# Step 0 of a convolution and MLP kernel: weight blocks rounded once and copied between partitions, their split moved behind the first product

## The chip, the core and the metric

The kernel runs on one core of one Trainium2 chip. The metric is the device time of one execution in microseconds. The core's engines have an instruction stream each: PE multiplies matrices (and loads weights, PEld), DVE does vector arithmetic, ACT activations, scaled copies and copies out of PE's accumulators, POOL further vector work, and it issues software DMA transfers; SP issues hardware DMA transfers. Instructions of one stream start in order, so one that waits holds up all behind it.

## The reference

Two layers: a causal convolution of 7 taps along the sequence, whose taps are a softmax over each head's weights, then an MLP of two products with a sigmoid-approximated GELU between them, all in float32.

```python
w = np.exp(weight - np.max(weight, axis=-1, keepdims=True))
w = w / (np.sum(w, axis=-1, keepdims=True) + 1e-09)          # (8 heads, 7 taps)
x = np.einsum('hk,bskhg->bshg', w, x_unf).reshape(B * S, D)  # B = 8, S = 4096, D = 192
h = x @ w_in                                                 # (32768, 192) @ (192, 2048)
g = h * (1.0 / (1.0 + np.exp(-1.702 * h)))
out = g @ w_out                                              # (32768, 2048) @ (2048, 192)
```

## The kernel before

**Steps.** The 32768 tokens go through in 32 steps of 1024 (`big` 0 to 31), each two sequences of 512 tokens, laid out in two halves of 256 (`o` = 0 and 1). The 192 channels are three chunks of 64 (`NC`, the index `k` or `c`); half 0 of the tokens has its channels on partitions 0 to 63, half 1 on 64 to 127 (`halves[o]`). So each weight that multiplies both halves must stand on both sets of partitions. The 2048 hidden columns are 16 blocks of 128 (`NF`, the index `r` or `i`), two neighbouring ones a pair (`N_W` = 8 pairs, index `j`).

**What a step does.** `transpose_x` (L143, DVE) brings x to channel-major, `conv` (L160 and L162, DVE) sums the taps into `own`. `hidden` runs 16 *units*, one for each block r: `unit` makes block r of the first product in a PE slot, `gelu` (L240, ACT) empties it into `g`; four slots are there. Then the second product turns `g` into the output, DVE transposes it (`turn`), SP stores it (L496).

**Steps 1 to 31.** A unit is three passes (`pass_of`, L209) of six matmuls on values split in parts: `xh` with `wh`, `xl` with `wl` (even r) or a ring slot (odd r), `xd` with a ring slot. `wh` and `wl` stay in SBUF; the other three of each pair are read back from `w_dram` into seven ring slots by SP (`load_ring`, L196) in every step. The second product of these steps (`second`) is a scheme with fewer products on sums of blocks (a hand-written list, `PLAN`); it needs sums and differences of blocks of w_out: the *forms*, 25 of them, 17 not being blocks themselves.

**Step 0** does plain float32 products and prepares all that. `split` (L387 to L391: two TENSOR_SCALAR of DVE, two activations of ACT) takes a loaded piece of a weight apart into words, `round_w_in` and `round_w_out` (L395, L398, L406, DVE) put it together rounded. A piece is 128 x 768 words: a pair of blocks of w_in, or four blocks of w_out. In the loop over `i` of `first_step`, after each `plain(slot, ...)` (L233, six matmuls), the next pair is rounded, then the last one split: `split_w_in` (L427 on ACT gives `wh`, L428 on POOL the rest), `split_rest` (L433 on DVE gives `wl` and a ring slot, L436 on POOL two more ring slots, L438 on SP writes the three slots to `w_dram`). As the ring is also where the parts are staged, a slot is free again only when its write has landed. `second_plain` (L499) is the second product of step 0, 48 rows of eight matmuls from `w_out_s`; behind each row it calls `at(row)`, into which the conv of step 1 (in `own`, which is free when the first product ends) and the forms are put. The forms: `add_forms` copies blocks on ACT (L296 and its neighbours) and lets POOL add others to them by accumulating DMAs (L298); `end_forms` turns four signs on ACT (L302). After `second_plain` come unit 0 of step 1, the output of step 0, and `hidden` of step 1. With the copies out of `second_plain`'s slots (L516, ACT) its slots come free.

**Order.** Nothing is scheduled: each engine runs its instructions in the order in which this code writes them, and a tile framework adds the waits that the data need. On SP stand, in order: x of step 0, sixteen loads of w_in (two for each pair: the same rows to both halves of the partitions), x of step 1 (eight transfers), pieces of w_out and the writes of L438, the first seven ring loads, x of step 2.

Raw words are loaded where there is room before the first step needs it: `raw` (in `g`, `osbs`, `room`), `raw_out` (`room`, `osbs`), and the words that are being rounded stand in four `sets` of the forms' tile.

Of the kernel before, what the change touches and what calls it, by code (L numbers as in the profile page):

```python
# [8 lines left out]
F32 = mybir.dt.float32  # L9
# [7 lines left out]
def kernel(  # L17
# [9 lines left out]
    nc = tc.nc  # L27
# [120 lines left out]
    def conv_src(c, k):  # L148
        return xt[:, c, :, Q - PAD + k : Q - PAD + k + T]
# [4 lines left out]
    def own_of(c):  # L154
        return own[:, 2 * c : 2 * c + 2, :]

    def conv(c, k, times=vec.tensor_scalar_mul):
        src, dst, tap = conv_src(c, k), own_of(c), tap_of(c, k)
        if k == 0:
            times(dst, src, tap)  # L160
        else:
            vec.scalar_tensor_tensor(  # L162
                out=dst, in0=src, scalar=tap, in1=dst, op0=ALU.mult, op1=ALU.add
            )

    def split_high(b0, b1):
        act.mul(xh[:, b0:b1, :], own[:, b0:b1, :], NEAR)

    def split_low(b0, b1):
        vec.scalar_tensor_tensor(  # L170
            out=xl[:, b0:b1, :], in0=own[:, b0:b1, :], scalar=UP, in1=wide(xh[:, b0:b1, :]),
            op0=ALU.mult, op1=ALU.subtract,
        )

    def split_both(b0, b1):
        vec.tensor_sub(xd[:, b0:b1, :], wide(xh[:, b0:b1, :]), own[:, b0:b1, :])
# [3 lines left out]
    wh = consts.tile([P, NF, NC, P], F32R)  # L180
# [5 lines left out]
    w_dram = dram.tile([STREAM, P, NC * P], F32)  # L186

# [18 lines left out]
    def pass_of(slot, w, t, first=False, last=False):  # L206
        for k in KS:
            for o in range(2):
                nc.tensor.matmul(  # L209
                    slot[o], w[halves[o], k, :], t[halves[o], 2 * k : 2 * k + 2, :],  # L210
                    start=first and k == KS[0], stop=last and k == KS[-1], skip_group_check=True,
                )

    def upper_high(slot, r):
        pass_of(slot, wh[:, r], xh, first=True)

    def upper_low(slot, r, big):
        if r % 2:
            q = STREAM * big + place("l", r)
            pass_of(slot, in_ring(q), xl)  # L220
            later(q)
        else:
            pass_of(slot, wl[:, r // 2], xl)

    def lower(slot, r, big):
        q = STREAM * big + place("d", r)
        pass_of(slot, in_ring(q), xd, last=True)
        later(q)

    def plain(slot, w):  # L230
        for k in KS:
            for o in range(2):
                nc.tensor.matmul(  # L233
                    slot[o], w[halves[o], k, :], own[halves[o], 2 * k : 2 * k + 2, :],
                    start=k == KS[0], stop=k == KS[-1], skip_group_check=True,
                )
# [29 lines left out]
    def form(i):  # L266
# [8 lines left out]
    COPY_O = [  # L275
        [(10, 2), (16, 1), (17, 0), (18, 0), (8, 7), (9, 5), (11, 3, -1), (12, 6, -1)],
        [(13, 3), (14, 3), (15, 0), (19, 4), (20, 4), (21, 5), (22, 7)],
        [],
        [(23, 1), (24, 1)],
        [(1, 14), (7, 0, -1)],  # L280
    ]
    SUMS_O = [
# [5 lines left out]
    ]  # L288
    TURN_O = (9, 17, 20, 21)

    def add_forms(stage):
        for dst, src, *sign in COPY_O[stage]:
            if sign:
                act.mul(form(dst), form(src), -1.0)
            else:
                act.copy(form(dst), form(src))  # L296
        for dst, src in SUMS_O[stage]:
            nc.gpsimd.dma_start(out=form(dst), in_=form(src), accum_op=ALU.add)  # L298

    def end_forms():  # L300
        for i in TURN_O:
            act.mul(form(i), form(i), -1.0)  # L302
# [7 lines left out]
    at_room, at_osbs = ([t[:, 2 * PART * i : 2 * PART * (i + 1)] for i in range(n)] for t, n in ((flat_room, 3), (osbs, 1)))  # L310
    raw = [flat_g(r)[:, 2 * PART * i : 2 * PART * (i + 1)] for r in range(3) for i in range(2)]
    raw += at_osbs + at_room[0:1]
    raw_out = at_room + at_osbs
    sets = [flat_form[:, 2 * PART * i : 2 * PART * (i + 1)] for i in range(4)]
    words_in, words_out = sets[0:3], (sets[3], sets[0])
    assert 8 * PART <= FORMS * NG * HD
    diag = flat_room[:, 2 * PIECE : 2 * PIECE + 2 * K * P].rearrange("p (c k q) -> p c k q", c=2, k=K)
# [19 lines left out]
    def load_w_in(j):  # L337
        for o in range(2):
            nc.sync.dma_start(
                out=raw[j][halves[o], :].bitcast(U32).rearrange("p (k f) -> p k f", k=NC), in_=w_in_v[j]  # L340
            )
# [7 lines left out]
    load_w_in(0)  # L349
    for j in range(1, N_W):  # L350
        load_w_in(j)
# [26 lines left out]
    def in_part(j):  # L378
        return raw[j], words_in[j % 3]

    def out_piece(i):
        return raw_out[i], words_out[(1, 0, 1, 0)[i]]
# [32 lines left out]
    def round_w_in(j):  # L415
        piece = in_part(j)
        join(piece)
        lo, hi, m, e = words(piece)
        rounded(piece, [(lambda a: a, m.bitcast(F32))])

    def w_of(j, what="w"):
        lo, hi, m, e = words(in_part(j))
        t = (m if what == "w" else e).bitcast(F32)
        return t.rearrange("p (k r f) -> p r k f", k=NC, r=2)

    def split_w_in(j):
        act.mul(wh[:, 2 * j : 2 * j + 2], w_of(j), DOWN)  # L427
        nc.gpsimd.tensor_sub(w_of(j, "rest"), w_of(j), wide(wh[:, 2 * j : 2 * j + 2]))  # L428

    def split_rest(j):  # L430
        lows = wl[:, j], in_ring(place("l", 2 * j + 1))
        for h in range(2):
            vec.tensor_scalar_mul(lows[h], w_of(j, "rest")[:, h], C)  # L433
        for h in range(2):
            r = 2 * j + h
            nc.gpsimd.tensor_sub(in_ring(place("d", r)), wide(lows[h]), wide(wh[:, r]))  # L436
        for q in range(3 * j, 3 * j + 3):
            nc.sync.dma_start(out=w_dram[q], in_=wide(in_ring(q)).rearrange("p k f -> p (k f)"))  # L438
# [134 lines left out]
    def second(big, bx, bs, by, more, next_first):  # L573
# [53 lines left out]
        def if_more(split):  # L627
            if more:
                split(0, 2 * NC)
# [18 lines left out]
    def first_step(tiles):  # L648
# [13 lines left out]
        act.copy(own_of(1), pairs[1][0].rearrange("p (n t) -> p n t", n=2))  # L662
        act.copy(own_of(2), pairs[1][1].rearrange("p (n t) -> p n t", n=2))
        load_x(1)
        for i in (1, 2):
            load_w_out(i)

        for i in range(NF):
            slot = tiles[i % 4]
            j = i // 2  # L670
            plain(slot, w_of(j)[:, i % 2])
            if i % 2 == 0:
                if j + 1 < N_W:
                    round_w_in(j + 1)
                split_w_in(j)
                if j + 2 < N_W:
                    split(in_part(j + 2))
                if i == 12:
                    load_w_out(3)
                if i == 14:  # L680
                    split(out_piece(1))
                    load_w_out(0)
            else:
                split_rest(j)
                if i == 15:
                    split(out_piece(2))
                if i in (7, 9, 11):
                    transpose_x(1, (i - 7) // 2)
            gelu(slot, i)

        pf, pa, pb, pc = tiles[3], tiles[1], tiles[0], tiles[2]

        for q in range(STREAM, STREAM + RING):
            load_ring(q)
        round_w_out(1)
        split(out_piece(3))
        round_w_out(2)
        split(out_piece(0))
        round_w_out(3)
        round_w_out(0)  # L700
        load_x(2)

        n_last = 3 * NG * NG - 1

        def at(i):
            if i == 0:
                for c in range(NC):
                    conv(c, 0, times=act.mul)
                for c in range(NC):
                    for k in range(1, K):  # L710
                        conv(c, k)
                split_high(0, 2 * NC)
                split_low(0, 2 * NC)
                split_both(0, 2 * NC)
                for c in range(NC):
                    transpose_x(2, c)
            if i == 2:
                add_forms(0)
            if i == 10:
                add_forms(1)  # L720
            if i == 20:
                add_forms(2)
                add_forms(3)
            if i == n_last:
                add_forms(4)
                end_forms()
# [62 lines left out]
```

## Time and profile before

| | |
|---|---|
| time, median of 3 runs | 2220.69 us (2220.56 to 2221.07) |
| the profiled execution | 2219.38 us, of which the profile's span 2217.7 us |
| mean granted PE clock | 0.991 |
| PE busy | 2181.6 us, 98% of the span |
| PEld | 1519.3 us, 69% |
| DVE | 1793.5 us, 81% |
| ACT | 1004.9 us, 45% |
| POOL | 376.6 us, 17% |
| software DMA queue / hardware DMA queue | 31.9% / 30.0% of 16 engines' span |
| chain that ended last | PE 93%, DMA 3%, DVE 1%, POOL 1% |

Busy shares are means over the whole span; of its 40 slices of 55.4 us the first has PE at 7 tenths, the next two at 8, all others at 9 or more. In rows of instructions, "L233" is line 233 of the kernel, `out<-in` the names of what is written and read, then sizes, then how many alike in a row; in brackets the idle time of the engine before them and what ended it. A row of a stretch gives, for each engine, busy time and number of instructions.

### The profile page before, as it was taken

How to read it: one execution, taken by the hardware profiler on the slowest of the kernel's cores; microseconds unless marked ns; L12 is line 12 of the kernel's file. 1: busy time of each engine (PE TensorE's matmuls, PEld its weight loads, DVE VectorE, ACT ScalarE, POOL GpSimd, SP SyncE). 2: the span in 40 equal slices, each digit the busy share in tenths (PEclk: the TensorE clock that was granted, in tenths of full speed). 3: DMA queues.
4: the chain of work that ended last, by engine and by line, in shares of the span. 5: the costliest groups of instructions: out<-in, count | busy, mean ns of one | idle time of the engine just before them, and what ended most of it. 6: DMA issues, size and time to landing. Idle time of an engine off the chain costs nothing.

```text
span 2217.7 us, 66206 instructions
## 1 busy us (share of the span) xinstructions
PE 2181.6 (98%) x28898; PEld 1519.3 (69%) x28898; DVE 1793.5 (81%) x2488; ACT 1004.9 (45%) x2133; POOL 376.6 (17%) x478
## 2 busy tenths in 40 slices
PE   7889999999999999999999999999999999999999
PEld 3457677766677766677766677766777766777766
DVE  7948888888888888888888888888888888888856
ACT  4444444444444444444444444444444444444443
POOL 3441111111111111011111011111011111011000
PEclk8899999999999999999999999999999999999999
DMA  9486575656575666575656575666575665675554
GB/s 226 134 167 154 126 183 150 163 144 145 137 184 147 164 146 149 135 180 148 166 145 144 143 178 147 165 148 142 144 175 147 166 146 139 152 174 147 137 120 98
DMA packets 269633, 338.41 MB, mean 153 GB/s; under 512 B 121504, under 2 KB 231520, under 8 KB 269344
## 3 DMA queue, kind: packets, MB, share of 16 engines
q0 software_dynamic: 44656, 144.19, 31.9%
q1 hardware_dynamic: 223040, 189.61, 30.0%
q8 instruction: 226, 3.70, 0.7%
q10 hardware_dynamic: 1648, 0.39, 0.1%
q14 instruction: 63, 0.52, 0.1%
HBM read 202.57 MB, written 29.88 MB: 105 GB/s over the span
## 4 chain that ended last, share of the span: by engine, by line
PE 93%; DMA 3%; DVE 1%; POOL 1%; issue 1%; SPq 0%; ACT 0%; POOLq 0%; DVEq 0%
PE slot L499 47%; PE slot L209 46%; DMA g<-in_moe_w_in_dram 1%; DVE own L162 1%; DMA w_form<-w_form 1%; DMA g<-in_x_dram 1%; POOL ring L436 0%; POOL w_form L428 0%; POOL w_form L298 0%; DMA w_dram<-ring 0%; DMA w_out_s<-w_form 0%; DVE w_form L398 0%; SPq L137 0%; DVE w_form L395 0%; DVE w_out_s L406 0%
## 5 line engine op out<-in xcount | busy, mean ns | idle before, releaser
L499 PE MATMUL slot<-g,w_form 128*32 128x256 f32 x8928 | 894.1, 379 | 0.0
L240 ACT ACTIVATE g<-slot 128x512 f32<-128x512 f32 x1024 | 555.9, 597 | 498.2 <-PE slot L209 497.0
L562 DVE TENSOR_TENSOR g<-g 128x1024 f32<-128x1024 f32 x403 | 483.6, 1219 | 210.1 <-ACT g L240 119.2
L499 PEld LDWEIGHTS slot<-g,w_form 128*32 128x32 f32 x8928 | 479.7, 110 | 138.4
L610 ACT COPY room<-slot 32x256 f32<-32x256 f32 x651 | 239.0, 367 | 626.7 <-PE slot L499 624.6
L499 PE MATMUL slot<-g,w_out_s 128*32 128x256 f32 (+1 forms) x6336 | 511.8, 394 | 5.2 <-ACT g L240 5.2
L209 PE MATMUL slot<-xh,wh 64*128 64x512 f32 x2976 | 426.2, 390 | 9.1 <-ACT room L516 9.1
L209 PE MATMUL slot<-xd,ring 64*128 64x512 f32 x2976 | 421.4, 387 | 0.0
L499 PEld LDWEIGHTS slot<-g,w_out_s 128*32 128x32 f32 x6336 | 265.6, 110 | 201.6 <-issue 13.9
L162 DVE SCALAR_TENSOR_TENSOR own<-xt,cw,own 128x512 f32<-128x512 f32 x564 | 377.8, 736 | 0.7
L209 PEld LDWEIGHTS slot<-xh,wh 64*128 64x128 f32 x2976 | 279.9, 184 | 78.9 <-issue 13.2
L209 PEld LDWEIGHTS slot<-xd,ring 64*128 64x128 f32 x2976 | 282.3, 184 | 58.1
L567 POOL DMA_DIRECT2D g<-g x124 | 118.2, 954 | 756.3 <-PE slot L499 515.5
L499 PE MATMUL slot<-osbs,w_form 128*32 128x256 f32 x2232 | 225.3, 379 | 0.0
L137 POOL DMA_DIRECT2D g<-in_x_dram x232 | 152.6, 686 | 389.6 <-PE slot L499 384.3
L209 PE MATMUL slot<-xl,ring 64*128 64x512 f32 x1488 | 211.2, 387 | 0.0
L209 PE MATMUL slot<-xl,wl 64*128 64x512 f32 x1488 | 210.6, 386 | 0.0
L499 PE MATMUL slot<-room,w_form 128*32 128x256 f32 x2232 | 171.5, 379 | 0.0
L209 PEld LDWEIGHTS slot<-xl,ring 64*128 64x128 f32 x1488 | 141.5, 185 | 29.1
L209 PEld LDWEIGHTS slot<-xl,wl 64*128 64x128 f32 x1488 | 140.8, 184 | 29.7
L499 PEld LDWEIGHTS slot<-osbs,w_form 128*32 128x32 f32 x2232 | 117.4, 110 | 42.6
L562 DVE TENSOR_TENSOR room<-slot,room 96x256 f32<-96x256 f32 x248 | 100.1, 414 | 57.2 <-PE slot L499 55.0
(87 smaller groups left out, 1431.2 us busy)
## 6 DMA issues: line engine op xcount, KB each, us to landing
ring<-w_dram SPq DMA_DIRECT2D x744, 192.0 KB, 2.7
g<-g POOLq DMA_DIRECT2D x124, 512.0 KB, 6.9
g<-in_x_dram POOLq DMA_DIRECT2D x220, 180.0 KB, 4.9
out_dram<-osbs SPq DMA_DIRECT2D x186, 128.0 KB, 5.6
g<-osbs POOLq DMA_DIRECT2D x31, 512.0 KB, 5.7
g<-room POOLq DMA_DIRECT2D x31, 512.0 KB, 6.7
g<-in_moe_w_in_dram SPq DMA_DIRECT2D x12, 384.0 KB, 11.3
w_dram<-ring SPq DMA_DIRECT2D x24, 192.0 KB, 2.0
```

What stands on the lines that cost most here:

```text
L137: queue.dma_start(out=xin[q0 : q0 + Q, n, j:NJ, :], in_=x_v[n, p, t : t + (NJ - j) * Q, v * Q : v * Q + XW].rearrange("(j i) d -> i j d", ...
L162: vec.scalar_tensor_tensor(out=dst, in0=src, scalar=tap, in1=dst, op0=ALU.mult, op1=ALU.add)
L209: nc.tensor.matmul(slot[o], w[halves[o], k, :], t[halves[o], 2 * k : 2 * k + 2, :], start=first and k == KS[0], stop=last and k == KS[-1], ...
L240: act.activation(g[:, r // NG, :, o, r % NG, :], slot[o].rearrange("p (n t) -> p n t", n=2), AF.Gelu_apprx_sigmoid,)
L499: nc.tensor.matmul(dst, w, t, start=first, stop=last, skip_group_check=True)
L562: (eng.tensor_add if op == "+" else eng.tensor_sub)(v(dst), v(a), v(b))
L567: nc.gpsimd.dma_start(out=spot(dst), in_=spot(a), accum_op=ALU.add)
L610: act.copy(to, d)
```

## The change

It rewrites the preparation in step 0; steps 1 to 31 keep their instructions, but for the place of two forms.

- **Loads.** w_in comes in ten loads instead of sixteen. Pairs 0 and 1 go to both halves of the partitions as before. Of pairs 2 and 3 one goes to the lower half, one to the upper; likewise 4 and 5, 6 and 7 (`IN_PARTS`). Three pieces of w_out follow at once, then x of step 1, the last piece, x of step 2.
- **Rounding.** So five pieces of w_in are split and rounded instead of eight. `round_w_in` then copies them by POOL's DMAs into `wh`: the whole piece to the first pair's place, and for a mixed piece its two halves, crossed, to the second pair's: eleven copies. Half 1 of the tokens finds a block of pairs 2 to 7 in the other place of its two (`at_slot`). Products 0 to 3 read the rounded words, products 4 to 15 read `wh`.
- **The split** into parts leaves the loop of the first product. It runs in `at(0)`, behind the first row of `second_plain`, in other functions: `top` (ACT), `rest` (DVE, instead of POOL), `spread` (ACT, instead of DVE), `differ` (DVE, instead of POOL), a chain of two buffers (`temps`, `rests`). The parts still pass through ring slots; their writes to `w_dram` are 42, as the crossed pairs go in halves. The first seven ring loads come behind them.
- **The conv of step 1** is done at product 13 into `early` (in `osbs`) instead of `own`, and split from there.
- **The forms** are single DVE instructions with other pairs of blocks: 19 in `at(0)` behind the split and x(2)'s transposes, two more at unit 6 of step 1. POOL's accumulating DMAs and ACT's copies and turns are gone.

```diff
+    def high_at(s):
+        return wh[:, s // 2, :, s % 2, :]
+    def at_slot(o, r):
+        return r if o == 0 or r < NG else r ^ 2
...
-    def add_forms(stage):
-        for dst, src, *sign in COPY_O[stage]:
...
-            nc.gpsimd.dma_start(out=form(dst), in_=form(src), accum_op=ALU.add)
+    def add_form(dst, a, op, b):
+        if op == "--":
+            vec.scalar_tensor_tensor(
+                out=form(dst), in0=form(a), scalar=-1.0, in1=form(b), op0=ALU.mult, op1=ALU.subtract
+            )
+        else:
+            (vec.tensor_add if op == "+" else vec.tensor_sub)(form(dst), form(a), form(b))
...
+    IN_PARTS = [(0, 0), (1, 1), (2, 3), (4, 5), (6, 7)]
+    SETS = (3, 2, 0, 1, 3, 2, 0, 1, 3)
...
+    for i in range(N_IN):
+        load_w_in(i)
+    for i in range(3):
+        load_w_out(i)
...
+    def round_w_in(i):
+        piece, (j0, j1) = in_part(i), IN_PARTS[i]
         join(piece)
         lo, hi, m, e = words(piece)
         rounded(piece, [(lambda a: a, m.bitcast(F32))])
+        nc.gpsimd.dma_start(out=wide(pair_of(j0)), in_=m.bitcast(F32))
+        if j0 != j1:
+            for o in range(2):
+                nc.gpsimd.dma_start(
+                    out=wide(pair_of(j1)[halves[1 - o], :]), in_=m.bitcast(F32)[halves[o], :]
+                )
-    def split_w_in(j):
-        act.mul(wh[:, 2 * j : 2 * j + 2], w_of(j), DOWN)
-        nc.gpsimd.tensor_sub(w_of(j, "rest"), w_of(j), wide(wh[:, 2 * j : 2 * j + 2]))
...
+    def top(j):
+        act.mul(temps[j % 2], wide(pair_of(j)), DOWN)
+    def rest(j):
+        vec.tensor_sub(rests[j % 2], wide(pair_of(j)), wide(temps[j % 2]))
+    def spread(j):
+        lows = wl[:, j], stage(3 * j + 1)
         for h in range(2):
-            vec.tensor_scalar_mul(lows[h], w_of(j, "rest")[:, h], C)
+            act.mul(lows[h], half(rests[j % 2], h), C)
+        act.copy(pair_of(j), wide(temps[j % 2]))
+    def differ(j):
+        lows = wl[:, j], stage(3 * j + 1)
         for h in range(2):
...
+            vec.tensor_sub(stage(3 * j + 2 * h), wide(lows[h]), half(wide(temps[j % 2]), h))
+        for e in range(3):
...
+                for o in range(2):
+                    nc.sync.dma_start(out=w_dram[3 * js[o] + e][halves[o]], in_=src[halves[o]])
...
+        split(in_part(2))
+        round_w_in(1)
         load_x(1)
-        for i in (1, 2):
-            load_w_out(i)
+        load_w_out(3)
+        early = osbs[:, 0 : 2 * NC * T].rearrange("p (b t) -> p b t", t=T)
+        work = {
+            0: lambda: (split(in_part(3)), round_w_in(2)),
+            1: lambda: (split(in_part(4)), round_w_in(3)),
+            3: lambda: (split(out_piece(0)), round_w_in(4)),
+            5: lambda: ([transpose_x(1, c) for c in range(NC)], split(out_piece(1)), round_w_out(0)),
+            7: lambda: (split(out_piece(2)), round_w_out(1)),
+            8: lambda: (split(out_piece(3)), round_w_out(2)),
+            10: lambda: round_w_out(3),
+            13: lambda: [conv(c, k, early) for k in range(K) for c in range(NC)],
+        }
         for i in range(NF):
...
+            plain(tiles[i % 4], i, half(words(in_part(i // 2))[2].bitcast(F32), i % 2) if i < NG else None)
+            if i in work:
+                work[i]()
+            gelu(tiles[i % 4], i)
...
         def at(i):
             if i == 0:
+                top(0)
+                split_high(early)
+                rest(0)
+                top(1)
+                spread(0)
+                split_low(early)
+                rest(1)
+                split_both(early)
+                differ(0)
+                for j in range(2, N_W):
+                    top(j)
+                    spread(j - 1)
+                    rest(j)
+                    differ(j - 1)
+                spread(N_W - 1)
+                differ(N_W - 1)
+                for q in range(STREAM, STREAM + RING):
+                    load_ring(q)
                 for c in range(NC):
                     transpose_x(2, c)
+                for item in FORMS_O:
+                    add_form(*item)
...
+            if (big, i) == (1, 6):
+                for item in LATE_FORMS_O:
+                    add_form(*item)
```

Three places show how the streams change. The first is ACT in the first product. `g<-slot` are the GELUs, two for each product (one for each half of the tokens), `w_form<-w_form,bias` the activations of a `split`, `wh<-w_form` the high part of a pair. Before, around products 4 and 5:

```order
L427 ACTIVATE wh<-w_form 128x768
L390 ACTIVATE w_form<-w_form,bias 128x768
L391 ACTIVATE w_form<-w_form,bias 128x768
L240 ACTIVATE g<-slot_65 128x2x256
L240 ACTIVATE g<-slot_66 128x2x256
L240 ACTIVATE g<-slot_71 128x2x256
L240 ACTIVATE g<-slot_72 128x2x256
```

The same place after the change:

```order
L243 ACTIVATE g<-slot_65 128x2x256
L243 ACTIVATE g<-slot_66 128x2x256
L383 ACTIVATE w_form<-w_form,bias 128x768
L384 ACTIVATE w_form<-w_form,bias 128x768
L243 ACTIVATE g<-slot_71 128x2x256
L243 ACTIVATE g<-slot_72 128x2x256
```

The high parts are gone from between the GELUs, and the two activations of a split, here that of w_out's second piece, now stand between the GELUs of products 4 and 5. The second place is DVE's stream at the same point. `xt<-g` are the transposes of x(1), `w_form<-room` and `w_form<-osbs` the words of pieces of w_out. Before, around product 7:

```order
L433 TENSOR_SCALAR wl<-w_form 128x384
L433 TENSOR_SCALAR ring<-w_form 128x384
L143 STREAM_TRANSPOSE xt<-g 128x576
L395 SCALAR_TENSOR_TENSOR w_form<-g,w_form 128x768
L398 SCALAR_TENSOR_TENSOR w_form<-g,w_form 128x768
L406 SCALAR_TENSOR_TENSOR w_form<-w_form 128x768
```

After, behind the rounding of w_in's last piece:

```order
L399 SCALAR_TENSOR_TENSOR w_form<-w_form 128x768
L143 STREAM_TRANSPOSE xt<-g 128x576 x3
L380 TENSOR_SCALAR w_form<-room 128x768
L381 TENSOR_SCALAR w_form<-room 128x768
L388 SCALAR_TENSOR_TENSOR w_form<-osbs,w_form 128x768
L391 SCALAR_TENSOR_TENSOR w_form<-osbs,w_form 128x768
L399 SCALAR_TENSOR_TENSOR w_out_s<-w_form 128x384 x2
```

The three transposes of x(1) stand together, at product 5 instead of products 7, 9 and 11, and the first words of w_out's second piece, which ACT's two activations read, come behind them. The third place is SP, from the loads of w_in to the first ring loads. Before:

```order
L339 DMA g<-in_moe_w_in_dram 64x3x512 x12
L339 DMA osbs<-in_moe_w_in_dram 64x3x512 x2
L339 DMA room<-in_moe_w_in_dram 64x3x512 x2
L137 DMA g<-in_x_dram 32x9x160 x8
L344 DMA room<-in_moe_w_out_dram 128x4x384 x2
L438 DMA w_dram<-ring 128x384 x18
L344 DMA osbs<-in_moe_w_out_dram 128x4x384
```

After:

```order
L331 DMA g<-in_moe_w_in_dram 64x3x512 x10
L336 DMA osbs<-in_moe_w_out_dram 128x4x384
L336 DMA room<-in_moe_w_out_dram 128x4x384 x2
L137 DMA g<-in_x_dram 32x9x160 x8
L336 DMA room<-in_moe_w_out_dram 128x4x384
L137 DMA room<-in_x_dram 32x9x160 x8
L452 DMA w_dram<-ring 128x384 x6
L455 DMA w_dram<-ring 64x384 x36
L199 DMA ring<-w_dram 128x384 x8
L513 DMA out_dram<-osbs 32x16x64 x6
```

x(1) now comes behind three pieces of w_out instead of ahead of two, six loads of w_in are gone ahead of it, and all writes to `w_dram` stand in one block behind the loads of x(2).

More of the change, by code (lines that the diff above doesn't have):

```diff
@@ L152, in tap_of, with own_of, conv @@
         return cw[:, c, k : k + 1]
[L154 to L158, printed above, removed]
+    def own_of(c, of=own):
+        return of[:, 2 * c : 2 * c + 2, :]
+    def conv(c, k, of=own):
+        src, dst, tap = conv_src(c, k), own_of(c, of), tap_of(c, k)
         if k == 0:
-            times(dst, src, tap)
+            vec.tensor_scalar_mul(dst, src, tap)
         else:
@@ L274 @@
     ]
[L275 to L280, printed above, removed]
-    ]
-    SUMS_O = [
[5 rows of a table removed]
-    ]
-    TURN_O = (9, 17, 20, 21)
-    def add_forms(stage):
-        for dst, src, *sign in COPY_O[stage]:
[L293 to L302, printed above, removed]
+    FORMS_O = [
[4 rows of a table added]
+    ]
+    LATE_FORMS_O = [(1, 14, "+", 22), (7, 0, "--", 21)]
+    def add_form(dst, a, op, b):
[5 more added lines that the diff above has]
+            (vec.tensor_add if op == "+" else vec.tensor_sub)(form(dst), form(a), form(b))
     NW = 4
@@ L628, in if_more @@
             if more:
-                split(0, 2 * NC)
+                split()
         ops = dict(
@@ L661, in first_step @@
         split(in_part(1))
-        act.copy(own_of(1), pairs[1][0].rearrange("p (n t) -> p n t", n=2))
-        act.copy(own_of(2), pairs[1][1].rearrange("p (n t) -> p n t", n=2))
+        for c in (1, 2):
+            act.copy(own_of(c), pairs[1][c - 1].rearrange("p (n t) -> p n t", n=2))
+        split(in_part(2))
+        round_w_in(1)
         load_x(1)
-        for i in (1, 2):
-            load_w_out(i)
-        for i in range(NF):
[L669 to L689, printed above, removed]
```

105 lines of the change are left out of this document (35 added, 70 removed), and 9 rows, old and new, of tables (FORMS_O, SUMS_O).

## The prediction

> **What bounds the kernel now.** I read the page first (PE busy 98%), then the stretches by time, then PE's instructions in order of time, last the chain of waits. The stretches of two later steps (columns: length, then busy time and count of PE, PEld, DVE, ACT, POOL, then granted clock, DMA share, GB/s):
>
> ```profile
> 148.20:215.00 66.80, 66.80 (x894) 49.57 (x896) 58.60 (x84) 31.64 (x68) 11.05 (x15) 0.97 0.65 156
> 1000.00:1066.80 66.80, 66.80 (x920) 47.11 (x916) 55.55 (x79) 30.39 (x66) 10.40 (x14) 1.00 0.62 153
> ```
>
> From 148.2 us on PE has no idle time, and the change leaves PE's instructions there as they are. What can be gained lies ahead of 148.19, in step 0 and the first units of step 1. PE's own rows there (start, length, count, idle before):
>
> ```profile
> 24.93 15.72 PE L233 MATMUL slot<-own,w_form 64*128 64x512 f32 x72
> 41.19 5.42 PE L233 MATMUL slot<-own,w_form 64*128 64x512 f32 x24 [0.54 <-DVE w_form L406]
> 54.57 13.25 PE L233 MATMUL slot<-own,w_form 64*128 64x512 f32 x48 [7.97 <-DVE w_form L406]
> 68.29 5.42 PE L233 MATMUL slot<-own,w_form 64*128 64x512 f32 x24 [0.47 <-DVE w_form L406]
> 75.96 7.12 PE L233 MATMUL slot<-own,w_form 64*128 64x512 f32 x24 [2.24 <-ACT g L240]
> 88.29 44.49 PE L499 MATMUL slot<-g,w_out_s 128*32 128x512 f32 x384 [5.21 <-ACT g L240]
> 132.70 0.97 PE L209 MATMUL slot<-xh,wh 64*128 64x512 f32 x6
> 138.28 0.84 PE L209 MATMUL slot<-xd,ring 64*128 64x512 f32 x6
> 148.19 2.25 PE L209 MATMUL slot<-xh,wh 64*128 64x512 f32 x6 [9.07 <-ACT room L516]
> 152.29 1.07 PE L209 MATMUL slot<-xh,wh 64*128 64x512 f32 x6
> ```
>
> The six idle times add up to 25.5 us, and the rows after them are slow: x48 took 13.25 where x72 took 15.72. Who was late, by the chain and by engine:
>
> ```profile
> 40.28 8.57 DMA w_dram<-ring
> 48.87 0.55 DVE L433 TENSOR_SCALAR ring<-w_form 128x384 fp32r<-128x384 f32 x1 [4.82 <-DMA w_dram<-ring]
> 51.99 2.44 DVE L406 SCALAR_TENSOR_TENSOR w_form<-w_form 128x768 f32<-128x768 f32 x1
> 59.65 2.49 POOL L428 TENSOR_TENSOR w_form<-w_form,wh 128x768 f32<-128x768 f32 x1 [0.99 <-ACT wh L427]
> 67.32 2.49 POOL L428 TENSOR_TENSOR w_form<-w_form,wh 128x768 f32<-128x768 f32 x1 [0.98 <-ACT wh L427]
> 74.98 2.50 POOL L428 TENSOR_TENSOR w_form<-w_form,wh 128x768 f32<-128x768 f32 x1 [0.98 <-ACT wh L427]
> 147.01 0.52 ACT L302 ACTIVATE w_form<-w_form 128x384 f32<-128x384 f32 x1 [4.96 <-DMA w_out_s<-w_form]
> 147.56 0.58 ACT L516 COPY room<-slot 96x512 f32<-96x512 f32 x1
> ```
>
> The 7.97 us are a ring slot whose write to DRAM stood behind the loads, then DVE's next block. After it the split of a pair of blocks goes round ACT, POOL and DVE once in 7.67 us (59.65, 67.32, 74.98), slower than PE's two products. The 9.07 us are the forms: ACT's sign turns wait for POOL's accumulating DMAs, and the copy that empties PE's slot stands behind them.
>
> **The floor.** With no waits and the full clock: 192 records of the plain products at 15.72/72 = 0.2183 us are 41.9, from 24.93 to 66.85. For the second product:
>
> ```profile
> 100.00:110.00 10.00, 10.00 (x97) 5.66 (x93) 9.61 (x14) 0.00 (x0) 0.00 (x0) 1.00 0.61 127
> 10.00:40.00 30.00, 30.00 (x98) 12.98 (x100) 25.95 (x32) 14.67 (x22) 9.32 (x6) 0.91 1.09 226
> 40.00:50.00 10.00, 6.07 (x28) 2.56 (x24) 5.15 (x7) 4.77 (x8) 3.85 (x3) 0.99 1.09 335
> 28.06 12.15 DMA g<-in_x_dram
> ```
>
> 384 records at 10.00/97 = 0.1031 are 39.6, to 106.44. Three units are nine passes, 0.68 apart ((138.28 - 132.70)/8 = 0.70, the first slower): 6.1. So r = 3 of step 1 could start at 112.6 instead of 148.19; 35.6 us are to be had.
>
> **What the change takes away.** The split of the blocks leaves the space between products, POOL does no arithmetic, no product waits for a ring slot, and the accumulating DMAs with ACT's turns are gone. So all six waits lose their cause. What comes instead:
>
> **Step 1's x comes late.** ACT now has the two activations of w_out's second piece ahead of the GELU of product 5, DVE has x(1)'s transposes ahead of that piece, and x(1) stands on SP behind three pieces of w_out. When does x(1) land? Before, SP's first write waits at 40.21 (28.06 + 12.15) for the transfer eight places ahead of it, which is x(1)'s third of eight. Five more of 184,320 B at the 226 GB/s of 10 to 40 us: 44.3. The change has six w_in transfers of 393,216 B fewer ahead (-10.4 us at 226) and three of w_out, 786,432 B each, more (+7.0 at the 335 of 40 to 50): 40.9. Then the new copies, five of 393,216 B and six of 196,608 B, 3.15 MB: nothing if they ride free, 9.4 us at 335; with everything at 226 they are 13.9 and w_out 10.4, so 58.2. The DMA share is 1.09 in both stretches, no engine is free, so I take three quarters of 9.4: x(1) at 48.0, bounds 40.9 and 58.2. Durations for what follows:
>
> ```profile
> 18.61 0.95 DVE L395 SCALAR_TENSOR_TENSOR w_form<-g,w_form 128x768 f32<-128x768 uint32 x1
> 21.34 0.56 DVE L387 TENSOR_SCALAR w_form<-g 128x768 uint32<-128x768 uint32 x1
> 87.62 1.03 DVE L406 SCALAR_TENSOR_TENSOR w_out_s<-w_form 128x384 f32<-128x384 f32 x2
> 116.21 1.75 DVE L176 TENSOR_TENSOR xd<-xh,own 128x1536 fp32r<-128x1536 f32 x1
> 150.56 12.01 DVE L162 SCALAR_TENSOR_TENSOR own<-xt,cw,own 128x512 f32<-128x512 f32 x18
> 162.49 2.09 DVE L143 STREAM_TRANSPOSE xt<-g 128x576 f32<-128x576 f32 x3
> 25.52 0.85 ACT L427 ACTIVATE wh<-w_form 128x768 fp32r<-128x768 f32 x1
> 26.32 0.94 ACT L390 ACTIVATE w_form<-w_form,bias 128x768 f32<-128x768 uint32 x1
> 28.13 1.06 ACT L240 ACTIVATE g<-slot 128x512 f32<-128x512 f32 x2
> 114.41 2.56 ACT L296 COPY w_form<-w_out_s 128x384 f32<-128x384 f32 x6
> ```
>
> DVE is there long before: from 26 us it has six TENSOR_SCALAR (0.5 each) and nine joins and roundings (0.9), so 37, or 38 with the wait for product 3. From x(1): transposes 2.09, TENSOR_SCALAR 0.56, two activations 1.9, half a GELU 0.5: 48.0 + 5.1 = 53.1. PE has a free slot until product 8 ends, 24.93 + 108 x 0.2183 = 48.5. **PE waits 4.6 us**, and runs slow after it: x48 took 13.25 instead of 48 x 0.2183 = 10.5 behind the 7.97 gap, so 2.8 more. Together 7.4. The wait of products 4 and 5 for their copies costs nothing beside it (at most a microsecond: rounded by 29.6, needed at 35.4), because what PE loses there it does not lose at product 9.
>
> **The second product's weights.** From 48.0: transposes 2.1, three splits of two TENSOR_SCALAR (2.9), four roundings of 0.9 + 0.9 + 1.03 (11.4): 64.4, ahead of 66.85 + 7.4 = 74.3. Hidden.
>
> **The conv in its own buffer** (3 + 18 instructions, 1.2 + 12.0): DVE to 77.6, beside PE's second product. Hidden.
>
> **The split behind the first product.** ACT: xh 1.5, then for each of eight pairs 0.85 + two of 0.43 + 0.85 = 2.6; DVE: a difference of 768 (0.95) and two of 384 (0.5); ACT waits for the first of these, so 2.9 a pair. With xl and xd (1.75 each) on DVE: 77.6 + 1.5 + 3.5 + 23.2 = 105.8. Then the last six of 42 writes and the ring's first load (issues by line: ns least, median, most, then from and to in us; of the load, us to landing):
>
> ```profile
> L438 SPq DMA_DIRECT2D w_dram<-ring x24: 319/320/1217, 40.3 to 85.5; - x24
> ring<-w_dram SPq DMA_DIRECT2D x8, 192.0 KB, 2.9
> L496 SPq DMA_DIRECT2D out_dram<-osbs x24: 315/516/1462, 135.5 to 348.4; - x24
> L298 POOL DMA_DIRECT2D w_form<-w_out_s x13: 1014/2149/3316, 115.5 to 136.8; - x13
> ```
>
> 6 x 0.32 + 2.9: 110.6. PE's first ring pass is at 106.44 + 7.4 + 1.36 = 115.2. Hidden with 4.6 us to spare, so a pair may take up to 3.5; past that every microsecond a pair costs eight.
>
> **The forms.** 19 on DVE at 0.5, behind x(2)'s transposes: 117.4, turns of 2.6, conv of step 2 13.2, two late forms 1.0, transposes 2.1: step 1's first sums at 136.3. PE's r = 4 is at 112.6 + 7.4 + 2.0 = 122.0, so 14.3 after it; before 12.2 (164.58 - 152.29, the transposes' end). Two microseconds later against a second half that waits for some of them: 0 to 2, I charge 1.0. SP sends the six stores of step 0 ahead of ring loads that r = 5 needs at 125.4; from 119 they take 3.1 at the median 0.516 and 8.8 at 1.46, plus 2.9: 125 to 131. I charge 1.0 of 0 to 5.
>
> **Sum.** r = 3 starts at 112.6 + 7.4 = 120.0 instead of 148.19: 28.2 us. It does not start slow any more (148.19 to 152.29 is 4.1 for a unit of 2.04): 2.1. Charged: 2.0. Gain 28.3. The profiled execution took 2219.38 us (span 2217.7): 2191.1. The median of the three runs, 2220.69, lies 1.31 above it, so **2192.4 us**.
>
> **Rivals.** *Copies ride free:* x(1) at 40.9 opens the GELU at 46.0, before PE needs it; no wait, no slow rows: 2185.0. Against it the DMA share of 1.09, for it that 226 and 335 GB/s differ while the share does not, so something else than the engines limits w_in. [...]
>
> *Copies cost in full, or are issued late:* x(1) at 58.2: PE waits 14.8 instead of 4.6, so 2202.6. A milder form: POOL's issue takes 3.3, the slowest L298, not one. Three issues from 29.6 end at 39.5, landed by 42; product 4 waits 6.5, product 9 no more, the slow rows stay: 9.3 for 7.4, so 2194.3. [...]
>
> *The split sets the end (slower):* a pair goes on at the 7.67 us of before, as a chain of ACT, DVE, ring slot and write. 82.6 + 61.4 + 4.8 = 148.8 for a pass due at 115.2: 33.6 lost and 2.8 of slow rows, 2228.8. It decides from 3.5 us a pair and eats the whole gain at 7.0. Against it: POOL's 2.5 us and DVE's stretched rows (2.44 for 0.96) made that pace, and both go.
>
> **How the numbers follow.** The forecast has 0.53 (2187 to 2197 by its charges), free copies 0.17, costly copies 0.21, the slow split 0.06, a part of it that eats the gain to within 0.2% (4.4 us, what a measurement tells from no change) 0.03. Faster 0.91, same 0.03, slower 0.06. The range takes in free and costly copies: 2184 to 2203.
>
> **What would show it.** Right: PE's one wait in step 0 stands before product 9, released by the GELU, some 5 us long; x(1)'s transposes wait for their DMA until about 48; the second product runs without idle; r = 3 starts near 120; the later steps keep their 66.7. Wrong: a wait before product 4 for the copies, PE waiting at the first ring pass, ACT and DVE past 3.5 us a pair, or a step that grew.

## The result, and the profile after

The changed kernel takes 2199.42 us (2197.24 to 2201.04, 4 runs), the kernel before 2220.88 on the same chip: 0.9903 of it, 95% interval 0.9886 to 0.992, 21.5 us less. The forecast was 2192.4, with 2184 to 2203: inside the range, 7 us short of the expected gain. The profiled execution took 2199.08 us, of which 2197.4 span; first its page's busy line, then PE's rows by time (start, length, count, idle before and what ended it):

```profile
PE 2176.1 (99%) x28898; PEld 1507.0 (69%) x28898; DVE 1783.0 (81%) x2505; ACT 999.8 (45%) x2125; POOL 329.4 (15%) x444
```

```profile
24.32 10.57 PE L236 MATMUL slot<-own,w_form 64*128 64x512 f32 x48
38.55 15.20 PE L236 MATMUL slot<-own,wh 64*128 64x512 f32 x60 [3.66 <-DMA wh<-w_form]
57.51 20.47 PE L236 MATMUL slot<-own,wh 64*128 64x512 f32 x84 [3.75 <-ACT g L243]
77.91 41.41 PE L516 MATMUL slot<-g,w_out_s 128*32 128x512 f32 x384
119.25 0.97 PE L212 MATMUL slot<-xh,wh 64*128 64x512 f32 x6
124.11 1.65 PE L212 MATMUL slot<-xd,ring 64*128 64x512 f32 x6 [3.20 <-DMA ring<-w_dram]
130.44 0.85 PE L212 MATMUL slot<-xh,wh 64*128 64x512 f32 x6
```

Three idle times are left, 10.6 us where there were 25.5: before product 4 for a copy of the weights, before product 9 for a GELU, and before step 1's first ring pass. The unit of r = 3 starts at 130.44, 17.75 us earlier than before; from there to the end of the span it is 2066.9 us (before: 2069.5). Who was late, on DVE and SP (SP's rows give start, issue time and count); then, in the view of the ring, the issues (ns least, median, most; first and last start); last, a piece of the chain of waits (start, length), the first ring load from its issue until it releases PE:

```profile
52.49 2.10 DVE L143 STREAM_TRANSPOSE xt<-g 128x576 f32<-128x576 f32 x3 [14.24 <-DMA room<-in_moe_w_out_dram]
81.60 0.95 DVE L436 TENSOR_TENSOR w_form<-wh,w_form 128x768 f32<-128x768 f32 x1
...
92.29 0.96 DVE L436 TENSOR_TENSOR w_form<-wh,w_form 128x768 f32<-128x768 f32 x1 [0.97 <-ACT w_form L433]
95.14 0.96 DVE L436 TENSOR_TENSOR w_form<-wh,w_form 128x768 f32<-128x768 f32 x1 [0.96 <-ACT w_form L433]
...
108.57 0.56 DVE L447 TENSOR_TENSOR ring<-ring,w_form 128x384 fp32r<-128x384 f32 x1 [3.14 <-DMA w_dram<-ring]
...
93.75 24.09 SPq L455 DMA_DIRECT2D w_dram<-ring  x36
117.89 8.22 SPq L199 DMA_DIRECT2D ring<-w_dram  x8
L452 SPq DMA_DIRECT2D w_dram<-ring x6: 320/380/402, 88.0 to 91.8; - x6
L455 SPq DMA_DIRECT2D w_dram<-ring x36: 445/586/1124, 93.7 to 117.2; - x36
117.89 6.09 DMA ring<-w_dram
```

x(1) opens DVE's transposes at 52.5: the trace has its last transfer landing at 52.2, while the load of w_out that the bracket names lands at 53.9, behind their start. Rounding and conv then fill DVE to 81.6, where the split begins. It keeps its pace, a pair every 2.85 us (92.29, 95.14), until it has to wait for ring slots whose writes SP has not yet sent (3.14 us at 108.57). SP is the late one: from 93.75 to 117.84 it does little but issue 36 writes of half a ring slot, 24.09/36 = 0.67 us each with the gaps, and the first ring load stands behind them. That load then takes 6.1 us. The copies, by their issues between 20 and 60 us (KB each, us to landing):

```profile
wh<-w_form POOLq DMA_DIRECT2D x5, 384.0 KB, 7.9
wh<-w_form POOLq DMA_DIRECT2D x6, 192.0 KB, 8.7
g<-in_x_dram SPq DMA_DIRECT2D x8, 180.0 KB, 19.1
```

### The profile page after: what moved, and what is told of

It reads as the page before. It is cut to its first block, busy times and chain, and to the rows that moved or that the text cites. A ratio compares the mean times of both kernels' runs of the same rounds, so it can differ in the third digit from the quotient of the medians.

```text
span 2197.4 us, 66177 instructions
## 1 busy us (share of the span) xinstructions
PE 2176.1 (99%) x28898; PEld 1507.0 (69%) x28898; DVE 1783.0 (81%) x2505; ACT 999.8 (45%) x2125; POOL 329.4 (15%) x444
## 4 chain that ended last, share of the span: by engine, by line
PE 94%; DMA 2%; DVE 2%; SPq 0%; ACT 0%; issue 0%; DVEq 0%; ACTq 0%
PE slot L516 48%; PE slot L212 46%; DMA g<-in_x_dram 1%; DVE osbs L162 1%; DMA room<-in_moe_w_out_dram 0%; DMA w_dram<-ring 0%; DMA g<-in_moe_w_in_dram 0%; DMA ring<-w_dram 0%; SPq L455 0%; DVE own L162 0%; DVE w_form L388 0%; DVE w_form L391 0%; SPq L137 0%; DVE xt L143 0%; ACT w_form L433 0%
## 5 line engine op out<-in xcount | busy, mean ns | idle before, releaser
L516 PEld LDWEIGHTS slot<-g,w_out_s 128*32 128x32 f32 x6336 | 254.1, 110 | 204.7 <-issue 39.8
L162 DVE SCALAR_TENSOR_TENSOR own<-xt,cw,own 128x512 f32<-128x512 f32 x546 | 364.5, 737 | 0.2
```

The source lines that it names most:

```text
L162: vec.scalar_tensor_tensor(out=dst, in0=src, scalar=tap, in1=dst, op0=ALU.mult, op1=ALU.add)
L516: nc.tensor.matmul(dst, w, t, start=first, stop=last, skip_group_check=True)
```

## The experiments

Each kernel differs from the changed one, unless it says otherwise, by the edit shown. "r = 3" is the start of step 1's fourth unit, which sums up all that stands ahead. The kernel before lay at 2219.4 to 2220.9 us from one set of runs to the next, so a gain over the changed kernel is read from the spans of the profiled executions (2197.4 for the changed kernel), and the times stand beside them. The four times of the changed kernel alone lie 3.8 us apart, so differences of 2 to 3 us (e1, e3) rest on what the rows show and not on the times.

**e1: whole writes.** Fourteen copies instead of eleven, so that every block stands in its own place on both halves and `w_dram` is written in 24 whole slots.

```diff
-        return r if o == 0 or r < NG else r ^ 2
+        return r
...
-        if j0 != j1:
...
+        if j0 == j1:
...
+        else:
+            for a, j in enumerate((j0, j1)):
+                for o in range(2):
+                    nc.gpsimd.dma_start(
+                        out=wide(pair_of(j)[halves[o], :]), in_=m.bitcast(F32)[halves[a], :]
+                    )
```

> Theory (SP's issues set the end of step 0's preparation): the changed kernel issues 36 half writes from 93.75 to 117.89 us, 0.64 us each with the gap, and the ring's loads stand behind them. With the crossed copies straightened, 24 whole writes of about 0.43 us are left, 1.3 us a pair against 2.9 for the split of a pair, so the writes end with the split near 108, the first ring load lands near 111 to 113, PE has no wait at the first ring pass (3.20 us before) and no slow rows behind it, and the unit of r = 3 starts near 125.5 instead of 130.44: about 5 us less, near 2194.5. Three more copies may add up to 1.5 us to the wait before product 4. Rival (the split itself or the landing of the writes is late, by traffic): the wait stays at about 3 us and the time at about 2199.

**e2: the same in halves.** The write's `if js[0] == js[1]:` becomes `if False:`.

> As e1, but every slot is written in two halves, 48 writes of the same bytes. Theory (issue cost by the number of writes): 48 at 0.64 us are 30.7 us, from 88 on to about 119, the first ring pass is at about 125 and the time 2199 to 2201, as in the changed kernel or a little later. Rival (what matters is the crossed place in memory or the bytes): as e1, near 2194.5.

2196.36 us (2195.83 to 2197.02) and 2201.72 (2201.47 to 2202.14). PE's passes and the writes of e1, then of e2:

```profile
122.40 0.86 PE L212 MATMUL slot<-xl,wl 64*128 64x512 f32 x6
123.09 0.85 PE L212 MATMUL slot<-xd,ring 64*128 64x512 f32 x6
127.86 0.84 PE L212 MATMUL slot<-xh,wh 64*128 64x512 f32 x6
L454 SPq DMA_DIRECT2D w_dram<-ring x24: 319/382/1138, 89.5 to 109.4; - x24
```

```profile
125.97 1.65 PE L212 MATMUL slot<-xd,ring 64*128 64x512 f32 x6 [3.43 <-DMA ring<-w_dram]
89.65 32.51 SPq L457 DMA_DIRECT2D w_dram<-ring  x48
L457 SPq DMA_DIRECT2D w_dram<-ring x48: 454/556/1464, 89.7 to 121.6; - x48
```

The same bytes in the same places are out by 110.5 in 24 issues and leave no wait; in 48 they take 32.5 us, 0.68 each, and the wait is back. So it is SP's time for the halves, and neither the crossed places nor the bytes, that makes the ring late: shown. e1 gains 2.1 us (span 2195.3) and not 5, because its first product ended later (second product at 80.26 instead of 77.91): behind waits of 3.10 and 4.04 us PE's rows of 60 and 84 records took 16.61 and 21.29 us there, against 15.20 and 20.47 behind 3.66 and 3.75 in the changed kernel, whose granted clock was 0.50 for 6.8 us of them. Why half a slot costs more to issue (0.59) than a whole one (0.38) stays open.

**e3: x(1) later on ACT.**

```diff
-            5: lambda: ([transpose_x(1, c) for c in range(NC)], split(out_piece(1)), round_w_out(0)),
-            7: lambda: (split(out_piece(2)), round_w_out(1)),
-            8: lambda: (split(out_piece(3)), round_w_out(2)),
-            10: lambda: round_w_out(3),
+            8: lambda: ([transpose_x(1, c) for c in range(NC)], split(out_piece(1)), round_w_out(0)),
+            9: lambda: (split(out_piece(2)), round_w_out(1)),
+            10: lambda: (split(out_piece(3)), round_w_out(2)),
+            11: lambda: round_w_out(3),
```

> x(1)'s transposes and the split of w_out's pieces 1 to 3 are moved from products 5, 7 and 8 to products 8, 9 and 10, so that the GELU of product 5 does not stand behind them on ACT. The wait of 3.75 us before product 9 should go, and most of the 2.4 us of slow rows behind it, so the first product ends 4 to 6 us earlier, at 72 to 74. Theory (the path goes over x(1)'s landing at 52.5, DVE's rounding and conv to 81.6, the split and SP's writes to 118): the ring is ready as late as before, the wait at the first ring pass grows from 3.2 to 7 to 9 us, r = 3 starts at 130 as before and the time stays within 1 us of 2199. Rival (PE's waits in the first product are on the path, as the prediction had it): 2193 to 2195.

2196.85 us (2196.14 to 2197.23). PE's rows, and SP's first ring load:

```profile
39.34 32.83 PE L236 MATMUL slot<-own,wh 64*128 64x512 f32 x142 [0.19 <-DMA wh<-w_form]
72.10 41.41 PE L516 MATMUL slot<-g,w_out_s 128*32 128x512 f32 x384
120.79 1.65 PE L212 MATMUL slot<-xd,ring 64*128 64x512 f32 x6 [5.70 <-DMA ring<-w_dram]
117.95 4.84 SPq L199 DMA_DIRECT2D ring<-w_dram  x8
```

The wait before product 9 goes and the first product ends 5.8 us earlier, but the wait at the ring grows from 3.2 to 5.7, and r = 3 is at 127.49: 2.9 us are left of 5.8 (span 2194.4). The load is issued when it was (117.95 against 117.89) and lands 3.3 us sooner, after 2.7 us instead of 6.1; POOL's last four loads of x(3), issued from 116.5 on in the changed kernel and from 110.7 on here, are the likely reason, not tried apart. So neither reading holds whole: the ring takes back half of what the first product gains, as the theory had it, but 2.9 us stay, where it had at most one.

**e4: the forms alone**, put into the kernel before: `FORMS_O` and `LATE_FORMS_O` behind x(2)'s transposes and at unit 6, nothing else.

> The kernel before with one part of the change alone: the forms as 21 DVE instructions instead of ACT's copies and turns and POOL's accumulating DMAs. Theory: the wait of 9.07 us before r = 3 of step 1 and the slow start behind it (2.1 us) go, r = 3 starts near 139 instead of 148.2, and the time is about 2209.5, half of the whole change's gain. Rival (something else stands right behind, such as the stores of step 0 or x(2)): only part of the 9.07 us goes and the time is 2213 to 2220.

2206.95 us (2206.81 to 2207.26) against 2219.41: 12.5 us. PE's rows there:

```profile
88.41 43.08 PE L486 MATMUL slot<-g,w_out_s 128*32 128x512 f32 x384 [6.91 <-ACT g L240]
131.42 0.96 PE L209 MATMUL slot<-xh,wh 64*128 64x512 f32 x6
135.65 0.84 PE L209 MATMUL slot<-xh,wh 64*128 64x512 f32 x6
```

The time is 2.5 us under the theory's: no unit waits any more, and r = 3 is at 137.69; the waits ahead of the second product are much as before (the last is 6.91 for 5.21).

**e12: the forms undone.** The changed kernel with `add_forms` and `end_forms` as they were, at rows 2, 10 and 20 and the last one of the second product.

> The changed kernel with the forms put back as before (ACT's copies, POOL's accumulating DMAs, ACT's turns), at the same rows of the second product. Theory (the forms and the rest are two paths side by side, and only both together pay): ACT comes to the first copies behind the split at about 111, the DMAs take as long as before, the turns hold the copies that empty PE's slots, and r = 3 starts at 143 to 148 again: 2211 to 2217, most of the gain lost, though the forms alone were worth 12.5 us. Rival (the parts add up): 2199.4 + 12.5 = 2212 with r = 3 near 143; or, if the DMAs are quicker beside an idle POOL, r = 3 at 135 to 140 and 2204 to 2209.

2221.79 us (2219.50 to 2223.36, 10 runs), 1.0007 of before with the interval 0.9998 to 1.0017. PE's rows, the last turn on ACT, and SP's writes:

```profile
134.51 1.65 PE L212 MATMUL slot<-xd,ring 64*128 64x512 f32 x6 [13.85 <-DMA ring<-w_dram]
149.01 2.25 PE L212 MATMUL slot<-xh,wh 64*128 64x512 f32 x6 [6.92 <-ACT room L546]
147.83 0.52 ACT L305 ACTIVATE w_form<-w_form 128x384 f32<-128x384 f32 x1 [5.46 <-DMA w_out_s<-w_form]
93.49 31.64 SPq L468 DMA_DIRECT2D w_dram<-ring  x36
```

Worse than either reading: r = 3 is at 149.01, later than before. PE is 13.7 us earlier at step 1 (118.99) and waits 20.8 us for the ring and for ACT's turns. The ring is late because SP's 36 writes take 31.6 us instead of 24.1: they take 0.45 to 2.06 us each to issue (the changed kernel: 0.45 to 1.12), while POOL's accumulating DMAs run beside them (a DMA share of 1.13 from 120 to 130 us). With the forms at these rows all the other edits together are worth nothing; other rows were not tried.

**e5: e1 and e3 together.**

> The edits of e1 and e3 together. Theory (two waits, each hiding the other: SP's writes behind the second product, and the GELU of product 5 behind x(1)): with both gone the first product ends near 72, the second near 113.5, and the ring's first load is issued with the split's end near 109 and lands near 112 to 114, so PE waits at most a microsecond there; r = 3 starts at 119 to 120.5 instead of 130.44, and the time is about 2188 to 2189.5: more than the sum of e1 (3.0) and e3 (2.6) under the changed kernel's 2199.4. Rival (DVE's chain from x(1) at 52 to the last write is the limit whatever SP does): the ring is ready near 118 and the time is 2193 to 2195.

2191.71 us (2191.18 to 2191.85): 7.4 us (span 2190.0), more than 2.1 + 3.0. r = 3 is at 120.08, as expected, but the time is 2.2 above its range: a new wait costs 1.6, in unit r = 5:

```profile
127.65 0.96 PE L212 MATMUL slot<-xd,ring 64*128 64x512 f32 x6 [1.59 <-DMA ring<-w_dram]
120.72 3.33 SPq L515 DMA_DIRECT2D out_dram<-osbs  x6
```

SP's stores of step 0 stand ahead of the next ring loads (e9 moves them).

**e6: the copies undisturbed.** x(1) and w_out's last three pieces are issued by POOL behind the last copy.

```diff
...
-            3: lambda: (split(out_piece(0)), round_w_in(4)),
+            3: lambda: (split(out_piece(0)), round_w_in(4), load_x(1, queue=nc.gpsimd), [load_w_out(p, nc.gpsimd) for p in (1, 2, 3)]),
...
```

> In the changed kernel x(1) and w_out's pieces 1 to 3 are issued by POOL behind the last copy instead of by SP, so that between 25 and 40 us the copies have the DMA engines nearly to themselves. Theory (the copies land 8 us after their issue because they share the engines with w_out and x(1)): they land in 3 to 4 us, the wait of 3.66 us before product 4 falls below 1 us, and x(1) lands at 47 to 50 instead of 52.5; the wait before product 9 stays, 2 to 5 us, as PE comes there earlier and x(1) earlier too. The ring is ready 2 to 4 us earlier, at 120 to 122: 2195 to 2198. Rival (a software DMA of this size is slow by itself): the wait before product 4 stays at 3 us or more, and x(1), in the same queue, lands later than 52.5: 2200 to 2204.

2198.52 us (2196.03 to 2199.64). The copies' issues, then PE's rows:

```profile
wh<-w_form POOLq DMA_DIRECT2D x5, 384.0 KB, 3.1
wh<-w_form POOLq DMA_DIRECT2D x6, 192.0 KB, 3.5
35.70 13.04 PE L236 MATMUL slot<-own,wh 64*128 64x512 f32 x60
56.44 20.46 PE L236 MATMUL slot<-own,wh 64*128 64x512 f32 x84 [7.70 <-ACT g L243]
122.82 1.65 PE L212 MATMUL slot<-xd,ring 64*128 64x512 f32 x6 [3.00 <-DMA ring<-w_dram]
```

The copies land in 3.1 to 3.5 us instead of 7.9 to 8.7, and product 4 waits for nothing: the cause was the loads beside them, and not the copies themselves. x(1) comes at 51.4, hardly earlier, and the wait of product 9 takes up the rest, 7.70 and not 2 to 5. The end is the ring's, as before, and the time 0.5 above its range.

**e7: e1, e3 and e6 together.**

> The edits of e1, e3 and e6 together. Theory: no wait at product 4 or 9, the first product ends at 66 to 68, the second at 107 to 109.5; x(1) at 47 to 50 sets DVE's chain, the ring is ready at 109 to 113, PE waits 0 to 3 us there, r = 3 at 114 to 119: 2184 to 2188. Rival as in e6: PE waits for copies and x(1), 2188 or more, not better than e5.

2189.86 us (2188.71 to 2191.94), 1.9 above its range: r = 3 at 117.76 is as expected, but a ring pass at 125.82 then waits 2.42 us, the one that e5 showed. The first product ends at 70.1 and not at 66 to 68: it still waits for GELUs, 0.84, 0.41 and 0.41 us.

**e8: e5, and x(1) ahead of w_out's pieces 1 and 2 on SP.**

```diff
-    for i in range(3):
-        load_w_out(i)
+    load_w_out(0)
...
-        load_w_out(3)
+        for i in (1, 2, 3):
+            load_w_out(i)
```

> e5, and on SP x(1) stands ahead of w_out's pieces 1 and 2. Theory (x(1) waits behind 1.57 MB, 4 to 5 us at 335 to 400 GB/s): x(1) lands near 48 and DVE's transposes start there, but the next instruction, the words of w_out's piece 1, now waits for that piece until 52 to 54, so the chain behind gains 0 to 2 us: 2187 to 2190. Rival (the engines are full and only the sum of bytes counts): x(1) stays at 51 or later.

2188.42 us (2188.04 to 2189.64). DVE and PE:

```profile
44.98 2.10 DVE L143 STREAM_TRANSPOSE xt<-g 128x576 f32<-128x576 f32 x3 [6.78 <-DMA g<-in_x_dram]
50.18 0.56 DVE L379 TENSOR_SCALAR w_form<-room 128x768 uint32<-128x768 uint32 x1 [3.10 <-DMA room<-in_moe_w_out_dram]
118.58 0.84 PE L212 MATMUL slot<-xh,wh 64*128 64x512 f32 x6
```

Span 2186.9, 10.5 us less than the changed kernel and 3.1 less than e5. x(1)'s transposes start 9.1 us earlier than in e5 (54.09) and the rival falls; DVE then waits for the piece of w_out, as expected, but has it at 50.2, where e5 starts on it at 56.1 and 52 to 54 were forecast. Of the 3.1 us, 1.5 stand ahead of r = 3; behind it the stores start at 116.3 instead of 120.7, and the wait that e5 showed is 0.65 instead of 1.59.

**e9: e8 with the stores later** (`store(0, n)` moved into step 1's `extra` at unit 3), **e10: e8 with w_out's pieces 1 to 3 issued by POOL behind the copies, e11: both.**

> e8, and the six stores of step 0 stand on SP behind five more ring loads (they are issued at r = 3 of step 1 instead of behind unit 0). Theory (SP waits there for DVE's turns of step 0, which stand behind the forms, and the ring loads wait behind SP: the wait of 0.65 us at 124.8 in e8, 1.59 in e5, 2.42 in e7): the wait goes, 0.6 to 1.5 us less than e8's 2188.4. Rival (the ring load is late by traffic): the wait stays.

> e8, and w_out's pieces 1 to 3 are issued by POOL behind the last copy instead of by SP behind x(1). Theory (the copies share the engines with what SP has issued): with x(1) alone beside them the copies of the third piece land in 4 to 6 us instead of 8, the wait of 2.86 us before product 4 falls to 0 to 1.5 us and the slow rows behind it go, w_out's piece 1 lands at 47 to 50; the first product ends at 66 to 68.5, the second near 108 to 110, where the ring is ready at 104 to 108: r = 3 at 114.5 to 116.5, and 2184.5 to 2187. Rival (as in e7, what PE wins in front it waits for at r = 5 and the forms): 2187.5 to 2189.

> e9's and e10's edits together. Theory: the sum of both, 2183 to 2186. Rival: DVE, with 19 forms, the turns, the conv and x(3)'s transposes behind the split, is late for the sums of step 1, which shows as waits of PE on DVE after 150 us: 2186 or more.

2189.04 us (2187.64 to 2189.59), 2189.16 (2188.14 to 2189.69) and 2188.19 (2187.59 to 2189.39): none can be told from e8. In e9 the ring wait went, and from r = 3 (120.26) to the end it is 2067.4 us, 0.9 less than e8's 2068.3; but the first product lost it again. PE's row of e9 ahead of the second product, then 41.4 to 44.8 us in e8 and in e9 (columns as in the prediction):

```profile
37.89 34.81 PE L236 MATMUL slot<-own,wh 64*128 64x512 f32 x144 [2.86 <-DMA wh<-w_form]
```

```profile
41.40:44.80 3.40, 3.40 (x19) 1.88 (x17) 0.00 (x0) 1.09 (x2) 0.00 (x0) 1.00 1.08 268
```

```profile
41.40:44.80 3.40, 3.40 (x12) 2.05 (x10) 0.00 (x0) 1.02 (x2) 0.02 (x1) 0.58 1.05 248
```

The same wait of 2.86 us, but e9 runs slow for one stretch more behind it (granted clock 0.58 for 1.00) and starts its second product 1.7 us later (72.63 for 70.94). In e10 the copies still took 7.8 us beside x(1) alone and the wait before product 4 was 2.75, so its theory falls. In e11 that wait, 2.92, is PE's only one: the 2183 to 2186 of its theory did not come, nor did the waits on DVE behind 150 us that its rival named.

## Why the prediction was right in sign and 7 us short

- **The bound, and where the gain lies: right.** The later steps kept their pace: 2066.9 us from r = 3 on against 2069.5, and most of the difference is the slow start of before, put at 2.1.
- **The floor: one term mis-sized.** I put the second product at 39.6 us, from 97 records in ten; it takes 41.41. A stretch counts each record that overlaps it, those across its edges too. +1.7 us.
- **x(1) late, GELU 5 behind it, PE waiting before product 9: right** in place and releaser. x(1) came at 52.2 for 48.0 (bounds 40.9 to 58.2), and the wait was 3.75 for 4.6.
- **The wait for the copies "costs nothing beside it": wrong.** The copies took 7.9 to 8.7 us to land and product 4 waited 3.66. Nor was it regained at product 9, since x(1) was late too. The first product took 53.6 us for the 49.3 forecast: +4.3. Of the rivals, free copies fell; that of copies issued late had the wait before product 4, but it comes from their landing (e6): POOL issued each in 0.5 to 0.8 us.
- **The split "hidden with 4.6 us to spare": the step that failed.** The pair's 2.9 us held: it is 2.85. But the writes were costed at 0.32 us from whole slots; halves cost 0.67 with the gaps, so SP needs 4.0 us a pair for six pairs, past the 3.5 that I had named as the point from which it decides. The first load was thus issued at 117.89, and it took 6.1 us where the 2.9 of before had been put in, a second mis-sized term: with 2.9 it would have landed at 120.8, when PE came for it (120.91). The ring's first pass ran at 124.11 for 115.2, and the three units took 11.2 us for 6.1: +5.1. So the wait of 3.2 us takes both. Without the halves it is gone (e1) and with more of them it is back though the load took 3.6 (e2): that part is shown. What slowed the load is not (see e3). The slow split was the right rival with the wrong engine: I had it as a chain at 7.67 us a pair.
- **The forms: right and undersold.** They are hidden. The 2.0 us charged for them and the stores did not come in the changed kernel, because r = 3 came 10 us later than forecast; with r = 3 at 118 to 120 the stores' part did in e5 (1.59) and e7 (2.42), less so in e8 (0.65).

From the start at 24.32, 0.6 us earlier than before, r = 3 is thus -0.6 + 4.3 + 1.7 + 5.1 = 10.5 us later than the 120.0 of the forecast, and 2.4 us come back behind it: 28.3 - 8.1 = 20.2, measured 20.3 between the two profiled executions. That the time still fell inside the range is partly luck: its upper end, 2203, was set for copies that cost in full, and half of the 10.5 us came from the writes and the load, for which the range had no room. These terms don't each name a gain: taking 5.8 us out of the first product gave 2.9 (e3), since the ring came next.

What the prediction did not see is how the parts hang together: the forms alone 12.5 us (e4), all the rest alone nothing (e12), both 21.5. It summed six waits on one engine; they belong to chains that run side by side and meet at the ring and at ACT's turns, and the later one sets the end.

e8, the simplest of the four best, which can't be told apart, is 0.9858 of before (interval 0.9841 to 0.9876; the changed kernel's is 0.9886 to 0.992), 10.5 us below the changed kernel by the spans.

## What to carry to other kernels

When a transfer is split in two, price the issues on the queue and not the bytes: here half a slot took longer to issue than a whole one (a median of 0.59 us against 0.38). Before adding up removed waits, ask which chain releases each and what stands next on it; undo one part, and do one alone, before crediting any. Count records in a long stretch from the first start to the last end, not in a window.

## What the runs showed of the hardware

Some short waits of PE cost more than their length here. Behind the waits of 3.66, 3.75 and 3.20 us in the changed kernel PE ran at half clock for one piece of 3.4 us each: the granted clock was 0.50 from 38.5 to 41.9, from 59.0 to 62.4 and from 123.8 to 127.2 us, and 1.00 behind each piece. Half of 3.4, an estimated 1.7 us, is lost for each. Behind the same wait of 2.86 us it was one piece in e8 (0.54 from 38.0 to 41.4, then 1.00) and two in e9 (0.50, then 0.58 from 41.4 to 44.8, then 1.00). Behind a wait of 2.24 us before product 14 such a piece came in the kernel before (0.50 from 77.1 to 80.5), where the next 24 records took 7.12 us; behind the same wait in e4 they took 5.42. In e7 the granted clock was 1.00 from 50 to 70 us, with three waits of 0.41 to 0.84 us in it. Whether this makes the spread of 3.8 us between the changed kernel's runs was not tried.
